# Batch 0's keys as fp32 through SyncE's queue, sums and products in PSUM tiles of their own, and a reordered Y0

## The chip, the cores and the metric

The kernel runs on one core of one Trainium2 chip. The metric is the device time of one launch in microseconds (us), the lower the better. Engines are named as in the profile: PE is TensorE, PEld its weight load, DVE is VectorE, ACT is ScalarE, POOL is GpSimd and SP is SyncE. DMAs are issued by POOL or by SP; the page shows them as queue q0 (software descriptors, from POOL) and q1 (hardware descriptors, from SP and ACT).

## What is computed

Linear attention with the feature map phi(x) = elu(x) + 1, followed by a two-layer block with a swish of learned slope.

```python
# q, k, v: (8 batches, 8 heads, 576 rows, 64), fp32
q_p, k_p = phi(q), phi(k)                      # phi(x) = x > 0 ? x + 1 : exp(x)
kv  = einsum('bhsd,bhse->bhde', k_p, v)
z   = sum(k_p, axis=2)
num = einsum('bhsd,bhde->bhse', q_p, kv)
den = einsum('bhsd,bhd->bhs', q_p, z)[..., None] + 1e-06
x   = (num / den), heads side by side           # 4608 tokens x 512
h   = x @ w_in                                  # w_in 512 x 2048
out = (h / (1 + exp(-beta * h))) @ w_out        # w_out 2048 x 512, out fp32
```

## The kernel before

Each of the 8 batches goes through phi, the products of keys and values, the normalised attention rows x, an H phase (x by w_in, 16 feature blocks, a Silu on ACT after each) and a Y phase (by w_out). A ninth pass takes the rows that the tiles of 512 tokens leave over. PE works through H and Y phases of 16 x 4 matmuls of 512 columns each; the attention of the next batch is woven in between. Only batch 0 has nothing to be woven into: its attention is the head of the kernel. Batch 1's attention is woven into batch 0's Y phase, here called Y0.

One batch of q, k or v is 8 x 576 x 64 numbers, that is 1.18 MB of fp32 in memory. A load by POOL into a bf16 tile casts on the way, so that it writes half as many bytes (576 KB) as it reads. The head:

```python
beta_row = consts.tile([FC, P], F32)
nc.sync.dma_start(out=beta_row, in_=moe_beta...)
nc.vector.memset(warm, 0.5)
nc.scalar.activation(tiny[:, 0:1], warm[:, 0:1], ACTF.Exp)   # brings the table in
for h0 in (0, 2): load(nc.gpsimd, xk[0], k, 0, h0, 2)        # k in two halves, cast to bf16
for h0 in (0, 2): load(nc.gpsimd, xq[0], q, 0, h0, 2)
for h0 in (0, 2): load(nc.gpsimd, vb[0], v, 0, h0, 2)
make_identity(nc, identity)                                  # on POOL
make_identity(nc, ident16)
# ... w_in in 4 loads by POOL; w_out 0 and 1 by SP, held until w_in 1 has landed;
# k, q, v of batch 1 by POOL, held until w_in 3 has landed;
# w_out 2 and 3 by SP into `stage`, held until q of batch 1 has landed
```

A "pair" (pr 0 or 1) is half of the heads, as the two loads bring them. phi is done by pairs: `phi_part` is the exponential on ACT, `phi_relu` is max(x, 0) + 1 on DVE, `phi_min` the minimum of both on DVE. `idle(n)` issues n matmuls of 512 columns on constants whose result is not used; they keep PE busy and its clock up.

```python
phi_step("k", 0, phi_part); phi_step("k", 1, phi_part)
idle(18)
bps = ...; nc.tensor.matmul(bps, beta_row, ident16, is_transpose=True, ...)
phi_step("k", 0, phi_relu); phi_step("k", 0, phi_min)
phi_step("q", 0, phi_part); phi_step("q", 1, phi_part, 0, 4); phi_step("q", 1, phi_part, 4, J)
phi_step("k", 1, phi_relu)
# beta_s, beta_m, beta_c, rbeta: five small DVE instructions
phi_step("k", 1, phi_min)
z_products(0, 0, kvz); idle(8); z_products(0, 1, kvz); idle(5)
phi_step("q", 0, phi_relu); phi_step("q", 0, phi_min)
phi_step("q", 1, phi_relu); phi_step("q", 1, phi_min, 0, 4); phi_step("q", 1, phi_min, 4, J)
q_trans0(0); q_trans0(1)
kv_direct(0, 0, kvz); z_evac(kvz)
for hh in range(2): kv_evac(0, hh, (0,), kvz)
q_trans0(2)
kv_direct(0, 1, kvz)
for hh in range(2): kv_evac(0, hh, (1,), kvz)
# ... denominators, numerators, x and its transposes, then H of batch 0
```

`z_products` sums phi(k) over its rows with 18 matmuls against ones, `kv_direct` makes phi(k) times v with 18 matmuls. Both write into the same two PSUM tiles `kvz`, in which each head has 64 columns of kv and one of z. The evacuations take them from there to SBUF under a mask.

Y0, with batch 1's attention and the start of batch 2's phi woven in:

```python
for i in range(2):
    for t in range(4): y_mm(0, t, i, yps[t])        # groups 0 and 1 of w_out
for pr in range(2): z_products(1, pr, kv1)
w_out_scale(2, 0); z_evac(kv1)                      # w_out 2 to bf16, scaled, four DVE instructions
# loads of q, k and v of batch 2, the first held until w_out 2 has landed
q_trans(1, tiles 0 to 3)
y_mm(0, 0, 2, yps[0]); q_trans(1, tile 4); y_mm(0, 1, 2, yps[1])
for pr in range(2): kv_direct(1, pr, kv1)
w_out_scale(3, 0)
for hh in range(2): kv_evac(1, hh, (0, 1), kv1)
# denominators; then numerators and transposes of x among y_mm(0, 2, 2) ... y_mm(0, 3, 3),
# with batch 2's phi on ACT and DVE between them
```

Of the kernel before, what the change touches and what calls it, by code (L numbers as in the profile page):

```python
# [8 lines left out]
F32 = mybir.dt.float32  # L9
BF16 = mybir.dt.bfloat16  # L10
# [6 lines left out]
def kernel(  # L17
# [10 lines left out]
    nc = tc.nc  # L28
# [44 lines left out]
        for a in vf  # L73
    ]

    def load(eng, dst, src, b, h0=0, n=4):

        rows = src[b].rearrange("h (g j) d -> (h g) (j d)", j=J)
        return eng.dma_start(  # L79
            out=dst[:, h0 : h0 + n].rearrange("p h j d -> p h (j d)"),  # L80
            in_=rows.rearrange("(i p) e -> p i e", p=P)[:, h0 : h0 + n],
        )
# [3 lines left out]


    beta_row = consts.tile([FC, P], F32)
    nc.sync.dma_start(out=beta_row, in_=moe_beta.rearrange("(c p) -> c p", p=P))
    nc.vector.memset(warm, 0.5)  # L90
    tiny = consts.tile([P, 2], BF16)
    nc.scalar.activation(tiny[:, 0:1], warm[:, 0:1], ACTF.Exp)
    for h0 in (0, 2):
        load(nc.gpsimd, xk[0], k, 0, h0, 2)
    for h0 in (0, 2):
        load(nc.gpsimd, xq[0], q, 0, h0, 2)
    for h0 in (0, 2):
        load(nc.gpsimd, vb[0], v, 0, h0, 2)
    identity = consts.tile([P, P], BF16)
    make_identity(nc, identity)  # L100
    ident16 = consts.tile([FC, FC], F32)
    make_identity(nc, ident16)

    w_in_v = moe_w_in.rearrange("(c p) f -> p c f", p=P)
    w_out_v = moe_w_out.rearrange("(c p) m -> p c m", p=P)
# [39 lines left out]
    def phi_part(b, a, pr, x, j0=0, j1=J):  # L145

        if j0 == 0:
            st[b, a, pr, "e"] = work.tile([P, 2, J, D], BF16, tag="e", name="e", bufs=3)
        nc.scalar.activation(st[b, a, pr, "e"][:, :, j0:j1], x[:, :, j0:j1], ACTF.Exp)  # L149
# [6 lines left out]
    def phi_tile(b, a):  # L156
        st[b, a] = work.tile([P, 2, J, P], BF16, tag=f"phi{a}", name=f"phi_{a}")
# [7 lines left out]
        )  # L165

    def xin(b, a, pr):
        return (xk if a == "k" else xq)[b % NX][:, 2 * pr : 2 * pr + 2]

    def v_copy(eng, b, pr):  # L170
# [15 lines left out]
                        start=(j == 0), stop=(j == J - 1), skip_group_check=True,  # L186
                    )

    def kvz_out(ps, pr):
        return ps[:, pr * 2 * EA : (pr + 1) * 2 * EA].rearrange("p (h e) -> p h e", h=2)  # L190

    def z_products(b, pr, ps):

        for j in range(J):
            for hh in range(2):
                r = slice(hh * G, (hh + 1) * G)
                nc.tensor.matmul(
                    kvz_out(ps[hh], pr)[:, :, D : D + 1],
                    st[b, "k"][r, pr, j, :], ones[r, :, None],
                    start=(j == 0), stop=(j == J - 1), skip_group_check=True,  # L200
                )

    def kv_direct(b, pr, ps):
        for j in range(J):
            for hh in range(2):
                r = slice(hh * G, (hh + 1) * G)
                nc.tensor.matmul(
                    kvz_out(ps[hh], pr)[:, :, 0:D],
                    st[b, "k"][r, pr, j, :], vb[b][r, 2 * pr : 2 * pr + 2, j, :],
                    start=(j == 0), stop=(j == J - 1), skip_group_check=True,  # L210
                )

    def kv_evac(b, hh, prs, ps):
        n = len(prs) * 2 * EA
        c = prs[0] * 2 * EA
        nc.vector.tensor_mul(
            st[b, "kv"][:, hh, prs[0] : prs[-1] + 1].rearrange("p a e -> p (a e)"),
            ps[hh][:, c : c + n],
            kvmask.rearrange("p a g e -> p (a g e)")[:, c : c + n],
        )  # L220

    def kv_tile(b):
# [120 lines left out]
    def mm_tile(name):  # L343
        return mmps.tile([P, 512], F32, tag="mm", name=name)

    def y_mm(b, t, i, yp, c0=0, c1=512):
        for c in range(4):
            ff = 4 * i + c
            nc.tensor.matmul(  # L349
                yp[:, c0:c1],  # L350
                g_sb[b % 2][:, ff, t * P : (t + 1) * P],
                w_out_sb[i][:, c, c0:c1],
                start=(ff == 0), stop=(ff == FC - 1), skip_group_check=True,
            )
# [40 lines left out]
    phi_tile(0, "k")  # L395
    phi_tile(0, "q")

    kvz = [mm_tile("kvz") for _ in range(2)]
    dps = mm_tile("dps")

    def misc_bf():
        return miscps.tile([P, 1024], BF16, tag="misc", name="tp")

    def z_evac(ps):
        for hh in range(2):
            nc.vector.tensor_mul(
                z0[:, hh],
                ps[hh][:, 0 : 4 * EA].rearrange("p (a h e) -> p a h e", a=2, h=2)[:, :, :, D],
                kvmask[:, :, :, 0],
            )  # L410
# [36 lines left out]
    def phi_step(a, pr, f, *r):  # L447
        f(0, a, pr, *((xin(0, a, pr),) if f is not phi_min else ()), *r)
# [4 lines left out]

    phi_step("k", 0, phi_part)
    phi_step("k", 1, phi_part)
    idle(18)
    bps = miscps.tile([P, FC], F32, tag="misc", name="bps")
    nc.tensor.matmul(bps, beta_row, ident16, is_transpose=True, start=True, stop=True)
    phi_step("k", 0, phi_relu)
    phi_step("k", 0, phi_min)  # L460
    phi_step("q", 0, phi_part)
    phi_step("q", 1, phi_part, 0, 4)
    phi_step("q", 1, phi_part, 4, J)
    phi_step("k", 1, phi_relu)
    nc.vector.tensor_copy(beta_s, bps)
    nc.vector.tensor_mul(beta_m, beta_s, beta_s)
    nc.vector.tensor_scalar(beta_m, beta_m, TINY * TINY, 2.0 * TINY, ALU.is_lt, ALU.mult)
    nc.vector.tensor_add(beta_c, beta_s, beta_m)
    nc.vector.reciprocal(rbeta, beta_c)
    phi_step("k", 1, phi_min)  # L470
    z_products(0, 0, kvz)
    idle(8)
    z_products(0, 1, kvz)
    idle(5)
    phi_step("q", 0, phi_relu)
    phi_step("q", 0, phi_min)
    phi_step("q", 1, phi_relu)
    phi_step("q", 1, phi_min, 0, 4)
    phi_step("q", 1, phi_min, 4, J)

    def q_trans0(t):
        q_trans(0, (t,), misc_bf()[:, 0 : 512 if t < NT - 1 else 256], (nc.scalar,))

    q_trans0(0)
    q_trans0(1)
    kv_direct(0, 0, kvz)
    z_evac(kvz)
    for hh in range(2):
        kv_evac(0, hh, (0,), kvz)
    q_trans0(2)  # L490
    kv_direct(0, 1, kvz)
    for hh in range(2):
        kv_evac(0, hh, (1,), kvz)
    dens(0, (0, 1), dps)
    recips(0, 2, P, dps)
    q_trans0(3)
# [32 lines left out]
    def w_out_scale(i, n_act):  # L529
        for c in range(4):  # L530
            ff = 4 * i + c
            if c < n_act:
                nc.scalar.mul(w_out_sb[i][:, c, :], w_out_f[i][:, c, :], rbeta[:, ff : ff + 1])
            else:
                nc.vector.tensor_scalar(  # L535
                    w_out_sb[i][:, c, :], w_out_f[i][:, c, :], rbeta[:, ff : ff + 1],
                    None, ALU.mult,
                )
# [10 lines left out]
    kv_tile(1)  # L549
    for pr in range(2):  # L550
        z_products(1, pr, kv1)
    w_out_scale(2, 0)
    z_evac(kv1)
    hold(load(nc.gpsimd, xq[2], q, 2), w_out2_dma)
    load(nc.gpsimd, xk[2], k, 2)
# [1 line left out]

    for ts in ((0, 1), (2, 3)):
        q_trans(1, ts, num0_tile().bitcast(BF16), (nc.scalar, nc.scalar))
    y_mm(0, 0, 2, yps[0])  # L560
    dps1 = num0_tile()
    q_trans(1, (4,), dps1.bitcast(BF16)[:, 512:768], (nc.scalar,))
    y_mm(0, 1, 2, yps[1])
    for pr in range(2):
        kv_direct(1, pr, kv1)
    w_out_scale(3, 0)
    for hh in range(2):
        kv_evac(1, hh, (0, 1), kv1)
# [5 lines left out]
    phi_part(2, "q", 0, xin(2, "q", 0))
    y_mm(0, 2, 2, yps[2])
    numer0(1, 0)
    numer0(1, 1)
    y_mm(0, 3, 2, yps[3])
    x_trans(1, 0, nc.scalar)
    phi_part(2, "q", 1, xin(2, "q", 1))  # L580
    numer0(1, 2)
    y_mm(0, 0, 3, yps[0])
    y_out(0, 0, yps[0])
    x_trans(1, 1, nc.scalar)
# [4 lines left out]
    numer0(1, 3)
    y_mm(0, 1, 3, yps[1])  # L590
    y_out(0, 1, yps[1])
    x_trans(1, 2, nc.scalar)
    phi_min(2, "q", 1)
    phi_part(2, "k", 1, xin(2, "k", 1))
    numer0(1, 4)
    y_mm(0, 2, 3, yps[2])
    y_out(0, 2, yps[2])
    x_trans(1, 3, nc.scalar)
# [91 lines left out]
```

## Time and profile before

| what | value |
|---|---|
| time, median of 3 runs | 297.33 us (296.52 to 297.83) |
| span of the profiled execution | 295.9 us |
| PE busy | 286.0 us, 97% |
| ACT busy | 159.8 us, 54% |
| DVE busy | 116.2 us, 39% |
| POOL busy | 35.2 us, 12% |
| mean granted clock of PE | 1.0 |

PE is counted as busy also in the idle matmuls, so a full PE isn't by itself a useful one: 30 records of them, 9.3 us, stand in the page's groups. The time of the head shows in where the first matmul of H stands, not in PE's share. The rates in GB/s count the bytes that a transfer writes: a casting load that writes 205 GB/s reads 410 GB/s.

### The profile page before, as it was taken

What the parts mean: (1) busy time and instruction counts of PE and PEld (TensorE: products, weight loads), DVE (VectorE), ACT (ScalarE), POOL (GpSimd) and SP (SyncE); (2) the same over time, 40 slices, a digit from 0 to 9 for tenths busy, and PEclk for the clock granted to TensorE, in tenths of its full rate; (3) what the DMA queues carried; (4) which work ended last, traced back from release to release, by engine and by line L of the source; (5) the groups of instructions that cost most, each with busy time, mean ns of one, the idle gap of its engine ahead of it and who ended that gap; (6) DMA issues with size and microseconds to landing.
All of it is one profiled execution on the core that took longest, in us unless ns stands there. A gap on an engine that the chain in (4) does not pass through costs nothing.

```text
span 295.9 us, 4697 instructions
## 1 busy us (share of the span) xinstructions
PE 286.0 (97%) x1855; PEld 143.4 (48%) x1884; DVE 116.2 (39%) x266; ACT 159.8 (54%) x208; POOL 35.2 (12%) x52
## 2 busy tenths in 40 slices
PE   8899989999999999999999999999999999999995
PEld 3484446455445544554455445544554444444443
DVE  3672367944453562265226532553251100110012
ACT  3648873966646790669067906691571068007500
POOL 8302012310022005000500053000000000000000
PEclk9999999999999999999999999999999999999999
DMA  7999999889679939961895189627122310131032
GB/s 89 194 207 337 208 298 172 181 207 223 88 162 283 168 33 231 261 102 40 219 267 97 30 216 263 114 21 177 38 55 50 82 37 0 35 73 35 0 71 74
DMA packets 51911, 40.24 MB, mean 136 GB/s; under 512 B 30752, under 2 KB 42800, under 8 KB 51888
## 3 DMA queue, kind: packets, MB, share of 16 engines
q1 hardware_dynamic: 39536, 26.50, 36.3%
q0 software_dynamic: 12192, 13.31, 27.5%
q8 instruction: 15, 0.25, 0.3%
q10 hardware_dynamic: 160, 0.13, 0.2%
q14 instruction: 8, 0.07, 0.1%
HBM read 36.71 MB, written 9.44 MB: 156 GB/s over the span
## 4 chain that ended last, share of the span: by engine, by line
PE 78%; DMA 14%; POOL 3%; ACT 2%; issue 1%; DVE 0%; SPq 0%; POOLq 0%; ACTq 0%
PE y_ps L349 37%; PE h_ps L331 36%; DMA w_in<-in_moe_w_in_dram 6%; DMA xq<-in_q_dram 5%; PE nps L282 3%; DMA stage<-in_moe_w_out_dram 2%; PE kvp L182 2%; ACT e L149 1%; DMA qTd<-phi_q 1%; POOL xk L79 1%; POOL w_in L107 1%; ACT xT L317 1%; POOL vf L79 0%; POOL xq L79 0%; ACT g L339 0%
## 5 line engine op out<-in xcount | busy, mean ns | idle before, releaser
L339 ACT ACTIVATE g<-h_ps,beta_c 128x512 bf16<-128x512 f32 x144 | 98.5, 688 | 100.1 <-PE h_ps L331 100.1
L349 PE MATMUL y_ps<-w_out,g 128*128 128x512 bf16 (+2 forms) x580 | 126.7, 373 | 2.1 <-DVE w_out L535 1.3
L331 PE MATMUL h_ps<-xT,w_in 128*128 128x512 bf16 (+1 forms) x545 | 116.5, 360 | 0.7 <-ACT xT L317 0.2
L349 PEld LDWEIGHTS <-g 128*128 128x128 bf16 x592 | 57.3, 98 | 66.6 <-issue 2.0
L331 PEld LDWEIGHTS <-w_in 128*128 128x128 bf16 x624 | 56.6, 98 | 58.6 <-issue 0.7
L361 DVE COPY y_sb<-y_ps 128x512 f32<-128x512 f32 (+2 forms) x37 | 24.8, 673 | 83.5 <-PE y_ps L349 78.4
L296 DVE TENSOR_TENSOR xs<-nps,rden 128x512 bf16<-128x512 f32 (+1 forms) x40 | 27.2, 687 | 5.7 <-DMA xT<-xs 3.3
L79 POOL DMA_DIRECT2D xk<-in_k_dram x9 | 7.0, 773 | 119.4 <-DMA qTd<-phi_q 71.9
L149 ACT ACTIVATE e<-xk 128x1152 bf16<-128x1152 bf16 x16 | 17.9, 1152 | 5.2 <-DMA xk<-in_k_dram 5.2
L149 ACT ACTIVATE e<-xq 128x1152 bf16<-128x1152 bf16 (+2 forms) x17 | 18.0, 1099 | 4.4 <-DMA xq<-in_q_dram 4.4
L160 DVE TENSOR_TENSOR phi_q<-e,r 128x1152 bf16<-128x1152 bf16 (+2 forms) x17 | 12.2, 721 | 15.4 <-ACT e L149 15.3
L231 DVE TENSOR_TENSOR kv_bd<-kvp,kvmask 128x260 bf16<-128x260 f32 x12 | 4.6, 423 | 26.4 <-PE kvp L182 26.4
L331 PE MATMUL h_ps<-xT_tail,w_in 128*128 128x512 bf16 x63 | 13.9, 379 | 0.1
L290 DVE TENSOR_SCALAR den<-nps 128x8 f32<-128x8 f32 (+1 forms) x30 | 4.9, 165 | 22.8 <-PE nps L282 22.8
L160 DVE TENSOR_TENSOR phi_k<-e,r 128x1152 bf16<-128x1152 bf16 x16 | 11.5, 748 | 4.1 <-ACT e L149 4.1
L282 PEld LDWEIGHTS <-qTd 128*128 128x128 bf16 x120 | 9.4, 98 | 7.3 <-DMA qTd<-phi_q 0.2
L282 PE MATMUL nps<-kv_bd,qTd 128*128 128x130 bf16 x120 | 12.1, 221 | 0.4
L172 POOL CAST vaug<-vf 128x1152 bf16<-128x1152 f32 x10 | 11.2, 1160 | 4.0 <-DMA vf<-in_v_dram 4.0
L138 PE MATMUL warm_ps<-warm 128*128 128x512 bf16 x30 | 9.3, 474 | 1.6 <-DVE warm L90 1.5
L153 DVE TENSOR_SCALAR r<-xk 128x1152 bf16<-128x1152 bf16 x16 | 7.6, 513 | 5.2 <-DMA xk<-in_k_dram 5.2
L149 ACT ACT_TABLE_LOAD x6 | 7.7, 1283 | 3.5 <-DMA xq<-in_q_dram 3.5
L339 ACT ACT_TABLE_LOAD x7 | 9.0, 1283 | 0.1
(63 smaller groups left out, 101.1 us busy)
## 6 DMA issues: line engine op xcount, KB each, us to landing
out_dram<-y_sb SPq DMA_DIRECT2D x70, 128.0 KB, 2.5
vf<-in_v_dram SPq DMA_DIRECT2D x5, 1152.0 KB, 7.6
xk<-in_k_dram POOLq DMA_DIRECT2D x7, 576.0 KB, 10.0
xq<-in_q_dram POOLq DMA_DIRECT2D x7, 576.0 KB, 12.8
w_in<-in_moe_w_in_dram POOLq DMA_DIRECT2D x4, 512.0 KB, 12.7
g<-in_moe_w_out_dram SPq DMA_DIRECT2D x2, 1024.0 KB, 9.2
stage<-in_moe_w_out_dram SPq DMA_DIRECT2D x2, 1024.0 KB, 8.3
vf<-in_v_dram POOLq DMA_DIRECT2D x2, 576.0 KB, 10.9
```

What stands on the lines that cost most here:

```text
L79: return eng.dma_start(out=dst[:, h0 : h0 + n].rearrange("p h j d -> p h (j d)"), in_=rows.rearrange("(i p) e -> p i e", p=P)[:, h0 : h0 + n],
L138: nc.tensor.matmul(warm_ps[:, 0:cols], warm[:, 0:P], warm[:, 0:cols], start=True, stop=True)
L149: nc.scalar.activation(st[b, a, pr, "e"][:, :, j0:j1], x[:, :, j0:j1], ACTF.Exp)
L153: nc.vector.tensor_scalar(r, x, 0.0, 1.0, ALU.max, ALU.add)
L160: nc.vector.tensor_tensor(st[b, a][:, pr, j0:j1].rearrange("p j (h d) -> p j h d", h=2), st[b, a, pr, "e"][:, :, j0:j1].rearrange("p h j d ...
L172: eng.tensor_copy(vaug[b % 2][:, pr, :, :, 0:D], src[:, 2 * pr : 2 * pr + 2].rearrange("p h j d -> p j h d"),)
L282: nc.tensor.matmul(nps[: qs.shape[-1], hh, pr * 2 * EA : (pr + 1) * 2 * EA], qs, st[b, "kv"][:, hh, pr, :], start=True, stop=True, skip_gr ...
L296: nc.vector.tensor_mul(xs[:n].rearrange("p i a d -> p a i d"), num, rd[:, :, :, None].to_broadcast([n, 2, 4, D]),)
L331: nc.tensor.matmul(hp[:, c0:c1], w_in_sb[ff // 4][:, kc, (ff % 4) * P : (ff % 4 + 1) * P], x[:, kc, c0:c1], start=(kc == 0), stop=(kc == K ...
L339: nc.scalar.activation(g_sb[b % 2][:, ff, :], hp, ACTF.Silu, scale=beta_c[:, ff : ff + 1])
L349: nc.tensor.matmul(yp[:, c0:c1], g_sb[b % 2][:, ff, t * P : (t + 1) * P], w_out_sb[i][:, c, c0:c1], start=(ff == 0), stop=(ff == FC - 1), ...
L361: nc.vector.tensor_copy(y_sb[:, c0:c1], yp[:, c0:c1])
```

## The change

Three parts.

1. Batch 0's k comes by SP's hardware queue, uncast, as fp32, into the space of `stage`, which is free until w_out 2 arrives. It is issued first of all SP's DMAs, ahead of beta. The exponential and the max of k read fp32. POOL makes the two identities first, then loads q, v and w_in. The aim is an earlier start of the data, with the descriptors of k made in a different place from those of q and v.
2. The sums of phi(k) and the two halves of kv are kept in separate PSUM tiles (two tiles for z, two for kv's first pair, two for its second), so that no product waits for an evacuation from the same tile. Idle matmuls become 14 + 4 + 10 in place of 18 + 8 + 5, and the small DVE work on beta stands elsewhere; the reciprocal of beta moves to just before w_out is scaled.
3. In Y0 the kv products of batch 1 come ahead of the third group of Y0, the group which is the first to need w_out 2. Behind it, the numerators and transposes come earlier, two of the eight scalings of w_out 2 and 3 go to ACT, two copies of transposed x go from ACT to DVE, and batch 2's phi comes after batch 1's transposes.

The diff, cut where marked:

```diff
+    k0f = stage[:, 0 : 4 * J * D].rearrange("p (h j d) -> p h j d", h=4, j=J)
@@
+    for h0 in (0, 2):
+        load(nc.sync, k0f, k, 0, h0, 2)
     nc.sync.dma_start(out=beta_row, ...)
     nc.vector.memset(warm, 0.5)
     nc.scalar.activation(tiny[:, 0:1], warm[:, 0:1], ACTF.Exp)
-    for h0 in (0, 2):
-        load(nc.gpsimd, xk[0], k, 0, h0, 2)
+    make_identity(nc, identity)
+    make_identity(nc, ident16)
     # q and v of batch 0, unchanged
-    make_identity(nc, identity)
-    make_identity(nc, ident16)
@@
     def xin(b, a, pr):
+        if b == 0 and a == "k":
+            return k0f[:, 2 * pr : 2 * pr + 2]
@@ z_products, kv_direct, kv_evac: other columns of other tiles; a cut @@
-    kvz = [mm_tile("kvz") for _ in range(2)]
+    kvp0 = [mm_tile("kvp0") for _ in range(2)]
@@
-    idle(18)
-    (transpose of beta)
+    idle(14)
     (phi of k and q: parts)
+    phi_step("k", 1, phi_min)
+    zt = [num0_tile() for _ in range(2)]
+    z_products(0, 0, zt)
+    (transpose of beta)
+    idle(4)
+    z_products(0, 1, zt)
     (beta_s, beta_m, beta_c)
-    nc.vector.reciprocal(rbeta, beta_c)
-    phi_step("k", 1, phi_min)
-    z_products(0, 0, kvz); idle(8); z_products(0, 1, kvz); idle(5)
     phi_step("q", 0, phi_relu)
+    z_evac(zt)
     (the rest of q's phi)
+    idle(10)
     q_trans0(0); q_trans0(1)
-    kv_direct(0, 0, kvz); z_evac(kvz)
-    (kv_evac of pair 0 from kvz)
+    kv_direct(0, 0, kvp0)
+    (kv_evac of pair 0 from kvp0)
     q_trans0(2)
-    kv_direct(0, 1, kvz)
+    kvp1 = [num0_tile() for _ in range(2)]
+    kv_direct(0, 1, kvp1)
@@ Y0 @@
-    w_out_scale(2, 0)            # was ahead of z_evac(kv1)
     q_trans(1, tiles 0 to 3)
-    y_mm(0, 0, 2, yps[0])
+    kv_direct(1, 0, kv1); kv_direct(1, 1, kv1)
+    w_out_scale(2, 0)
+    kv_evac(1, both, kv1)
     q_trans(1, tile 4)
-    y_mm(0, 1, 2, yps[1])
-    kv_direct(1, 0, kv1); kv_direct(1, 1, kv1)
-    w_out_scale(3, 0)
-    kv_evac(1, both, kv1)
+    y_mm(0, 0, 2, yps[0])
     (denominators of batch 1)
-    (batch 2's phi, numerators, x_trans 0 to 3 on ACT, the other y_mm, mixed)
+    y_mm(0, 1, 2, yps[1]); numer0(1, 0); numer0(1, 1)
+    w_out_scale(3, 2)            # two of the four on ACT
+    (y_mm, numerators and x_trans 0, 1 on ACT and 2, 3 on DVE; then batch 2's phi)
```

More of the change, by code (lines that the diff above doesn't have):

```diff
@@ L92 @@
     nc.scalar.activation(tiny[:, 0:1], warm[:, 0:1], ACTF.Exp)
-    for h0 in (0, 2):
-        load(nc.gpsimd, xk[0], k, 0, h0, 2)
+    identity = consts.tile([P, P], BF16)
+    make_identity(nc, identity)
+    ident16 = consts.tile([FC, FC], F32)
+    make_identity(nc, ident16)
     for h0 in (0, 2):
@@ L98 @@
         load(nc.gpsimd, vb[0], v, 0, h0, 2)
-    identity = consts.tile([P, P], BF16)
-    make_identity(nc, identity)
-    ident16 = consts.tile([FC, FC], F32)
-    make_identity(nc, ident16)
     w_in_v = moe_w_in.rearrange("(c p) f -> p c f", p=P)
@@ L187, in kv_products, with row_products @@
                     )
-    def kvz_out(ps, pr):
-        return ps[:, pr * 2 * EA : (pr + 1) * 2 * EA].rearrange("p (h e) -> p h e", h=2)
-    def z_products(b, pr, ps):
+    def row_products(b, pr, dsts, mov):
         for j in range(J):
@@ L197, in z_products, with z_evac @@
                 nc.tensor.matmul(
-                    kvz_out(ps[hh], pr)[:, :, D : D + 1],
-                    st[b, "k"][r, pr, j, :], ones[r, :, None],
+                    dsts[hh], st[b, "k"][r, pr, j, :], mov(r, j),
                     start=(j == 0), stop=(j == J - 1), skip_group_check=True,
                 )
-    def kv_direct(b, pr, ps):
[L204 to L211, printed above, removed]
+    def z_products(b, pr, ps):
+        row_products(b, pr, [a[:, 256 + 2 * pr : 258 + 2 * pr] for a in ps], lambda r, j: ones[r])
+    def z_evac(ps):
+        for hh in range(2):
+            nc.vector.tensor_mul(
+                z0[:, hh], ps[hh][:, 256:260].rearrange("p (a h) -> p a h", a=2),
+                kvmask[:, :, :, 0],
+            )
+    def kv_direct(b, pr, ps):
+        row_products(
+            b, pr, [a[:, pr * P : (pr + 1) * P].rearrange("p (h d) -> p h d", h=2) for a in ps],
+            lambda r, j: vb[b][r, 2 * pr : 2 * pr + 2, j, :],
+        )
     def kv_evac(b, hh, prs, ps):
-        n = len(prs) * 2 * EA
-        c = prs[0] * 2 * EA
+        p0, p1 = prs[0], prs[-1] + 1
         nc.vector.tensor_mul(
-            st[b, "kv"][:, hh, prs[0] : prs[-1] + 1].rearrange("p a e -> p (a e)"),
-            ps[hh][:, c : c + n],
-            kvmask.rearrange("p a g e -> p (a g e)")[:, c : c + n],
+            st[b, "kv"][:, hh, p0:p1].rearrange("p a (h e) -> p a h e", h=2)[:, :, :, 0:D],
+            ps[hh][:, p0 * P : p1 * P].rearrange("p (a h d) -> p a h d", a=p1 - p0, h=2),
+            kvmask[:, p0:p1, :, 0:D],
         )
@@ L402, in misc_bf @@
         return miscps.tile([P, 1024], BF16, tag="misc", name="tp")
[L404 to L410, printed above, removed]
     def dens(b, ts, dps):
@@ L455 @@
     phi_step("k", 1, phi_part)
-    idle(18)
-    bps = miscps.tile([P, FC], F32, tag="misc", name="bps")
-    nc.tensor.matmul(bps, beta_row, ident16, is_transpose=True, start=True, stop=True)
+    idle(14)
     phi_step("k", 0, phi_relu)
@@ L464 @@
     phi_step("k", 1, phi_relu)
+    phi_step("k", 1, phi_min)
+    zt = [num0_tile() for _ in range(2)]
+    z_products(0, 0, zt)
+    bps = miscps.tile([P, FC], F32, tag="misc", name="bps")
+    nc.tensor.matmul(bps, beta_row, ident16, is_transpose=True, start=True, stop=True)
+    idle(4)
+    z_products(0, 1, zt)
     nc.vector.tensor_copy(beta_s, bps)
@@ L468 @@
     nc.vector.tensor_add(beta_c, beta_s, beta_m)
-    nc.vector.reciprocal(rbeta, beta_c)
-    phi_step("k", 1, phi_min)
[L471 to L474, printed above, removed]
     phi_step("q", 0, phi_relu)
+    z_evac(zt)
     phi_step("q", 0, phi_min)
@@ L485 @@
     q_trans0(1)
-    kv_direct(0, 0, kvz)
-    z_evac(kvz)
+    kv_direct(0, 0, kvp0)
     for hh in range(2):
-        kv_evac(0, hh, (0,), kvz)
+        kv_evac(0, hh, (0,), kvp0)
     q_trans0(2)
-    kv_direct(0, 1, kvz)
+    kvp1 = [num0_tile() for _ in range(2)]
+    kv_direct(0, 1, kvp1)
     for hh in range(2):
-        kv_evac(0, hh, (1,), kvz)
+        kv_evac(0, hh, (1,), kvp1)
     dens(0, (0, 1), dps)
@@ L538, in w_out_scale @@
                 )
+    nc.vector.reciprocal(rbeta, beta_c)
     w_out_scale(0, 0)
@@ L559 @@
         q_trans(1, ts, num0_tile().bitcast(BF16), (nc.scalar, nc.scalar))
-    y_mm(0, 0, 2, yps[0])
+    for pr in range(2):
+        kv_direct(1, pr, kv1)
+    w_out_scale(2, 0)
+    for hh in range(2):
+        kv_evac(1, hh, (0, 1), kv1)
     dps1 = num0_tile()
     q_trans(1, (4,), dps1.bitcast(BF16)[:, 512:768], (nc.scalar,))
-    y_mm(0, 1, 2, yps[1])
-    for pr in range(2):
-        kv_direct(1, pr, kv1)
-    w_out_scale(3, 0)
-    for hh in range(2):
-        kv_evac(1, hh, (0, 1), kv1)
+    y_mm(0, 0, 2, yps[0])
     dens(1, range(NT), dps1)
@@ L571 @@
     recips(4, 5, G, dps1)
+    y_mm(0, 1, 2, yps[1])
+    numer0(1, 0)
+    numer0(1, 1)
+    w_out_scale(3, 2)
+    y_mm(0, 2, 2, yps[2])
+    x_trans(1, 0, nc.scalar)
+    numer0(1, 2)
+    y_mm(0, 3, 2, yps[3])
+    x_trans(1, 1, nc.scalar)
+    numer0(1, 3)
+    y_mm(0, 0, 3, yps[0])
+    y_out(0, 0, yps[0])
+    x_trans(1, 2, nc.vector)
+    numer0(1, 4)
+    y_mm(0, 1, 3, yps[1])
+    y_out(0, 1, yps[1])
+    x_trans(1, 3, nc.vector)
     phi_tile(2, "q")
     phi_tile(2, "k")
[L574 to L584, printed above, removed]
+    for pr in range(2):
+        phi_part(2, "q", pr, xin(2, "q", pr))
     for pr in range(2):
@@ L588 @@
     phi_part(2, "k", 0, xin(2, "k", 0))
[L589 to L592, printed above, removed]
+    y_mm(0, 2, 3, yps[2])
+    y_out(0, 2, yps[2])
     phi_min(2, "q", 1)
     phi_part(2, "k", 1, xin(2, "k", 1))
[L595 to L598, printed above, removed]
     y_mm(0, 3, 3, yps[3])
```

## The prediction

> **What bounds the kernel now.** I read the page first: PE's share, then the chain that ended last.
>
> ```profile
> PE 286.0 (97%) x1855; PEld 143.4 (48%) x1884; DVE 116.2 (39%) x266; ACT 159.8 (54%) x208; POOL 35.2 (12%) x52
> ...
> PE 78%; DMA 14%; POOL 3%; ACT 2%; issue 1%; DVE 0%; SPq 0%; POOLq 0%; ACTq 0%
> PE y_ps L349 37%; PE h_ps L331 36%; DMA w_in<-in_moe_w_in_dram 6%; DMA xq<-in_q_dram 5%; PE nps L282 3%; DMA stage<-in_moe_w_out_dram 2%; PE kvp L182 2%; ACT e L149 1%; DMA qTd<-phi_q 1%; POOL xk L79 1%; POOL w_in L107 1%; ACT xT L317 1%; POOL vf L79 0%; POOL xq L79 0%; ACT g L339 0%
> ```
>
> PE is 78% of the chain, in H and Y. The DMA part is 14%, about 41 us, and it lies at the front: the chain by time runs through the loads of w_in, q and w_out up to 49 us and then stays on PE. So there are two parts. From about 56 us on the kernel is PE's, and the change touches nothing there. Before that it is a race between one stream of DMAs and PE. The DMA view of the first 60 us, in 40 slices of 1.5 us, shows the stream:
>
> ```profile
> DMA  0199999999999999999999999899939999997558
> GB/s 0 15 171 185 71 167 194 207 205 205 208 210 204 206 206 295 365 405 383 232 207 205 209 207 207 219 401 314 370 119 104 200 204 208 207 219 215 137 126 204
> ```
>
> It is full from 3 us to about 40 us. Its casting loads write about 207 GB/s, and so read about 414; the uncast loads of w_out write up to 405. Both move the same bytes of memory in the same time, so fp32 instead of bf16 costs the stream nothing. The start is poor, as the windows of 1 us show (the last two numbers are the DMA share and GB/s):
>
> ```profile
> 2.00:3.00 1.00, 1.00 (x4) 0.31 (x3) 0.39 (x4) 0.22 (x2) 1.00 (x3) 1.00 0.24 14
> 3.00:4.00 1.00, 1.00 (x4) 0.31 (x3) 0.00 (x0) 0.00 (x0) 1.00 (x2) 1.00 1.04 152
> 4.00:5.00 1.00, 1.00 (x4) 0.45 (x3) 0.00 (x0) 0.00 (x0) 1.00 (x3) 1.00 1.17 195
> 5.00:6.00 1.00, 1.00 (x4) 0.30 (x2) 0.70 (x1) 0.78 (x1) 1.00 (x2) 1.00 1.23 188
> 6.00:7.00 1.00, 1.00 (x5) 0.44 (x4) 0.58 (x1) 0.39 (x1) 0.86 (x4) 1.00 1.18 75
> 7.00:8.00 1.00, 1.00 (x9) 0.40 (x9) 0.18 (x1) 0.00 (x0) 1.00 (x3) 1.00 0.87 96
> ```
>
> Nothing of size moves before about 2.8 us, though POOL issued k at 1.24, and from 6 to 8 us the rate falls to less than half. At 195 GB/s the hole loses (120 + 99)/195 = 1.1 us of the stream. The timeline shows what the head waits for:
>
> ```profile
> 8.59 1.16 ACT L149 ACTIVATE e<-xk 128x1152 bf16<-128x1152 bf16 x1 [2.21 <-DMA xk<-in_k_dram]
> ...
> 10.02 1.16 ACT L149 ACTIVATE e<-xq 128x1152 bf16<-128x1152 bf16 x1 [0.26 <-DMA xq<-in_q_dram]
> ...
> 12.45 0.87 DVE L160 TENSOR_TENSOR phi_q<-e,r 128x512 bf16<-128x512 bf16 x2
> 12.93 0.34 PEld L250 LDWEIGHTS <-phi_q 128*128 128x128 bf16 x6 [0.70 <-DVE phi_q L160]
> ...
> 18.30 1.05 PE L331 MATMUL h_ps<-xT,w_in 128*128 128x128 bf16 x16
> ...
> 43.51 0.77 PE L349 MATMUL y_ps<-w_out,g 128*128 128x512 bf16 x2 [1.06 <-DVE w_out L535]
> ```
>
> k's halves are usable at 5.2 and 8.6 us, q's from 10.0, q's phi lets PE transpose at 12.9, and H of batch 0 starts at 18.3. From there PE has few holes until Y0's third group waits for w_out 2; in windows of 1 us PE is busy 0.44, 0.47 and 0.78 between 42 and 45 us, so 1.3 us are lost there.
>
> **What the Trainium skill says.** "DMA: Bandwidth & Descriptors", section "SWDGE vs HWDGE vs iDMA": a cast is done only by GpSimd's queue, SP's can't. So k has to stay fp32 there, as the change does it. Its "Specifications" give a first byte after some 1 us for GpSimd's path and some 0.6 us for SP's. The trace agrees in direction: k is issued at 1.24 and moves from about 2.8; beta, issued by SP at 0.74, has bytes in the window 1 to 2 us and lands 1.6 us after its issue.
>
> "SBUF — State Buffer", section "SBUF: two separate sides": a DVE instruction in a two-port mode locks GpSimd out of its port, and a DMA by GpSimd then lacks descriptors, while SP's is immune. The hole at 6 to 8 us follows the first DVE work on k (5.22, 0.70 us, against 0.46 for the second of its kind) and POOL's making of the identities (5.64 to 7.23). I can't tell from this trace which of them made it.
>
> "VectorE: DVE Perf Modes", section "Mode 2×_2P": with one fp32 source in SBUF it makes two elements a cycle, where bf16 may reach four. The trace has a scaling of w_out, 512 fp32 elements, in 0.42 to 0.48 us; less about 0.15 us of fixed time, 1152 of them should take about 0.75 us, an estimate. Per pair of k that is 0.3 us more than 0.46. ACT's exponential takes 1.16 us for 1152 elements, and I take the same for fp32 (no fp32 exponential is in this trace).
>
> **Part 1: k by SP.** SP starts at 0.74 as it did for beta, so data from about 1.5 instead of 2.8 us: 1.3 us gained by the whole stream, as what follows is queued behind. q is still issued by POOL at about 2.8, since the identities (0.43 + 0.29 + 0.10 + 0.68 = 1.5 us) now take the place of k's two issues (1.55 us). Its packets start at about 4.4, when k's second half is ending. If the hole goes too, another 1.1 us is gained, plus what uneven engines lose in it: q's first half would land at 6.4 us (1.5, plus k and half of q, 1.77 MB at 410 GB/s = 4.3, plus 0.5 to be seen), against 10.0. If it stays, about 8.5. I give the two even chances, mean 7.4, and with it the stream ahead by 1.5 to 3.5 us.
>
> What the head makes of it is less, as DVE becomes the limit. Estimate, with k at 3.6 and 5.1: relu and min of pair 0 to 5.6, relu (0.75) and min (0.70) of pair 1 to 7.1. Beta's copy needs PE, which has 14 idle matmuls (cold 0.43 us each up to about 6.1, then 0.21) and the first sums to do: 7.6. Four beta instructions at 0.2: 8.4. relu of q 8.9, the z evacuations 9.2, min 9.9, relu 10.4, two min's of 0.44: 11.2. Before they ended at 13.3. So 2.1 us are gained without the hole, about 1.4 with it. PE arrives at the q transposes when 4 idle matmuls (0.86), the second sums (0.38) and 10 idle ones (2.1) are done, about 10.8: they just fit.
>
> **Part 2: own PSUM tiles.** The second kv half waited 0.19 us for an evacuation of the first; that and z's earlier evacuation are worth 0.2 to 0.3 us on this path. Sum for the start of H: 18.3 less about 2.0 = **16.3 us**. w_in 0 landed at 16.9 before, 9.7 us after its issue; with the stream ahead by 1.5 to 3.5 it is there by 13.4 to 15.4. w_out 0 and 1 (landed 27.8 and 30.4) are needed at 31.8 instead of 33.8, and come early too.
>
> **Part 3: Y0.** Before, PE finished its q transposes at 42.45 and waited for w_out 2 (landed 42.9, first scaling 0.5 later). After, everything up to there is 2.0 earlier, so 40.4; then 36 kv matmuls, 1.2 us, bring it to 41.6. w_out 2 lands at 42.9 less 1.5 to 3.5 = 39.4 to 41.4, its first quarter is scaled at 39.9 to 41.9. The wait is closed, or nearly so, and of the 1.3 us of hole about **1.0** is won. The numerators no longer stand behind four scalings of w_out 3 in DVE's queue (1.7 us), which keeps PE fed. Batch 2's phi, later on ACT, costs nothing I can find: its four exponentials (4.6 us) and a table load (1.28) end some 2 us after H of batch 1 begins, but PE has four PSUM tiles, 3.5 us of work, before it needs the first Silu.
>
> Sum: 2.0 + 1.0 = 3.0 us, and H of batch 1 starts at about 52.9 instead of 55.9. From there on 240 us of PE work are as before and shifted. 297.3 - 3.0 = **294.3 us**.
>
> **Rivals.** (1) *DVE or PE's idle matmuls take the place of the DMA.* The five phi and beta steps of DVE leave no gap by my count, and the ten idle matmuls sit right ahead of the transposes; each half microsecond that z's sums come later goes straight into the start of H. For it: DVE was busy 3.65 of 5 us from 10 to 15. It would halve the gain of part 1: 295.5. (2) *The stream stays as late as before*: SP's loads of k are slow at the start, or share with q so that q doesn't gain; then only 0.5 us comes from the head, and part 3 gives little, since w_out 2 is as late as ever: 296.5. Against it: SP's loads of w_out run at 365 to 405 GB/s. (3) *Given back later*: batch 2's transposed q (landed 64.7, with PE waiting 0.22 for it) and its products hang on loads held behind w_out 2 and on DVE, which was busy 5.0 of 5 us from 55 to 60. If they don't move with PE, H of batch 1 waits for them and 1 to 2 us are lost: 295.5 to 296. (4) *The hole goes and more holes close*: the head gains 3, Y0 1.5: 292.5.
>
> **Range and chances.** The middle is between the main reckoning and the rivals on its slow side, 294.4 us. The best case, (4), a little exceeded, sets the low end, 292.2; (2) with the spread of runs (0.5 us) the high end, 297.0. A gain over 2% needs 291.4 us, 6 us off a head in which the stream can give 3.5 and Y0 1.3: 0.03. A loss over 2% needs a new wait of 6 us in a part where nothing is added to PE: 0.02.
>
> **What would show it.** Step by step in the profile after: the first exponential of k at 3.6 to 4.2 us, and the second at about 5.2 to 5.5; relu of k at 0.75 us; no hole in GB/s at 6 to 8 us if the descriptors were its cause and are not disturbed anew; first exponential of q at 6.5 to 8.5; the first H matmul at 16.3; PE without a wait for w_out 2 at 41 to 43; H of batch 1 at 52.9; and from there equal lengths. It is wrong if the exponential of k waits beyond 5 us, if H of batch 0 starts after 17.5, or if the stretch from H of batch 1 to the end is longer by more than 0.5 us than before.

## The result and the profile after

| | before | changed |
|---|---|---|
| time, median of 4 runs | 297.51 us | 332.63 us |
| lowest to highest | 296.52 to 297.83 | 332.10 to 333.71 |
| ratio of the times | 1 | 1.119 (95% interval 1.115 to 1.123) |
| span of the profiled execution | 295.9 us | 330.5 us |
| mean granted clock of PE | 1.0 | 0.936 |

The changed kernel is 12% slower, where 1% faster was predicted. The page says at a glance where: these are PE, granted clock, DMA and rate over 40 slices of 8.3 us, and the busy totals.

```profile
PE 286.1 (87%) x1853; PEld 143.3 (43%) x1881; DVE 115.2 (35%) x266; ACT 159.3 (48%) x208; POOL 32.9 (10%) x50
...
PE   6000079999999999999999999999999999999995
...
PEclk9555559999999999999999999999999999999999
DMA  8999994000279679679918942991522221022013
GB/s 197 205 269 263 289 181 73 2 1 2 49 162 259 90 181 267 109 83 279 175 25 203 267 82 65 251 209 43 134 66 50 56 65 32 0 63 65 0 43 85
```

PE is busy for as long as before (286.1 and 286.0 us), so nothing was added to its work. From slice 2 to slice 5, about 8 to 41 us, it does nothing at all, and its clock is at 0.5 from there to slice 6. Meanwhile the loads run on, until at about 49 us nothing is left to move. The waits of the first 96 us name the cause (engine and line, what it waited for, us in total, times, longest):

```profile
ACT e L151 <- DMA stage<-in_moe_w_out_dram: 40.4, 2, 38.3
DVE r L155 <- DMA stage<-in_moe_w_out_dram: 39.4, 2, 38.1
PEld L197 <- DVE phi_k L162: 38.4, 2, 36.6
PE nps L197 <- DVE phi_k L162: 37.0, 2, 36.2
```

The exponential and the max of batch 0's *k* wait for a load of *w_out*. The timeline shows it with the times:

```profile
0.74 0.97 SPq L81 DMA_DIRECT2D stage<-in_k_dram  x2
...
34.35 0.92 SPq L114 DMA_DIRECT2D stage<-in_moe_w_out_dram  x2
40.55 1.16 ACT L151 ACTIVATE e<-stage 128x1152 bf16<-128x1152 f32 x1 [38.32 <-DMA stage<-in_moe_w_out_dram]
...
42.57 0.40 PE L197 MATMUL nps<-ones,phi_k 64*128 64x2 bf16 x18 [36.15 <-DVE phi_k L162]
...
43.80 1.16 ACT L151 ACTIVATE e<-stage 128x1152 bf16<-128x1152 f32 x1 [2.09 <-DMA stage<-in_moe_w_out_dram]
```

k was issued at 0.74 us, and its two loads landed 3.6 and 4.8 us after their issue. But k lies in `stage`, and `stage` is also where w_out 2 and 3 go. In the program text the two lines that load w_out 2 and 3 stand near the top, ahead of the lines of phi. A reader waits for the last writer ahead of it in the text. For k's readers that is not k's load but w_out's, which is itself held until q of batch 1 has landed. So the head of the kernel starts at 40.55 us, when w_out 2 is there, and its second pair at 43.80, when w_out 3 is.

It must also be said what is read then. w_out 2 covers columns 0 to 2047 of `stage`, w_out 3 the columns behind them, and k columns 0 to 2303, with its second pair from 1152 on. So, by these times, phi is taken of w_out's numbers in k's place from 40.55 us on, and what becomes batch 0's attention isn't that of its k. The same holds for experiments 4 and 5 below. The instructions and their shapes are the same ones, so the time can be read as the time of this order of waits.

Where the 34.6 us of span come from, by the first matmul of each H phase in the two timelines:

| stretch | before, us | changed, us | difference |
|---|---|---|---|
| start to H of batch 0 | 18.30 | 54.97 | +36.67 |
| H of batch 0 to H of batch 1 | 37.61 | 35.20 | -2.41 |
| H of batch 1 to the end | 240.0 | 240.3 | +0.3 |

All of the loss, and more, is in the head. Between the two H phases 2.41 us are won, and behind them the kernel is 0.3 us longer than before.

### The profile page after: what moved, and what is told of

It is laid out like the page before. It is cut to its first block, busy times and chain, and to the rows that moved or that the text cites. A ratio compares the mean times of both kernels' runs of the same rounds, so it can differ in the third digit from the quotient of the medians.

```text
span 330.5 us, 4700 instructions
## 1 busy us (share of the span) xinstructions
PE 286.1 (87%) x1853; PEld 143.3 (43%) x1881; DVE 115.2 (35%) x266; ACT 159.3 (48%) x208; POOL 32.9 (10%) x50
## 4 chain that ended last, share of the span: by engine, by line
PE 81%; DMA 12%; POOL 2%; ACT 2%; issue 1%; DVE 1%; SPq 0%; POOLq 0%; ACTq 0%
PE y_ps L354 37%; PE h_ps L336 35%; DMA w_in<-in_moe_w_in_dram 5%; DMA stage<-in_moe_w_out_dram 3%; DMA xq<-in_q_dram 3%; PE nps L287 2%; PE kvp L186 2%; DMA qTd<-phi_q 1%; PE warm_ps L140 1%; PE nps L434 1%; ACT g L344 1%; POOL w_in L109 1%; PE xtp L317 1%; PE kv L197 0%; POOL xq L81 0%
## 5 line engine op out<-in xcount | busy, mean ns | idle before, releaser
L197 PE MATMUL nps<-ones,phi_k 64*128 64x2 bf16 x36 | 0.8, 164 | 37.0 <-DVE phi_k L162 37.0
L151 ACT ACTIVATE e<-stage 128x1152 bf16<-128x1152 f32 x2 | 2.3, 1163 | 40.4 <-DMA stage<-in_moe_w_out_dram 40.4
L81 POOL DMA_DIRECT2D xk<-in_k_dram x7 | 5.2, 746 | 152.3 <-DMA qTd<-phi_q 134.9
L197 PEld LDWEIGHTS <-phi_k 64*128 64x128 bf16 x144 | 3.2, 96 | 39.1 <-DVE phi_k L162 38.4
L162 DVE TENSOR_TENSOR phi_q<-e,r 128x1152 bf16<-128x1152 bf16 (+2 forms) x17 | 12.1, 721 | 15.3 <-ACT e L151 15.2
L151 ACT ACTIVATE e<-xk 128x1152 bf16<-128x1152 bf16 x14 | 15.5, 1150 | 1.4 <-DVE phi_q L162 1.4
L155 DVE TENSOR_SCALAR r<-stage 128x1152 bf16<-128x1152 f32 x2 | 1.5, 760 | 39.4 <-DMA stage<-in_moe_w_out_dram 39.4
L140 PE MATMUL warm_ps<-warm 128*128 128x512 bf16 x27 | 10.4, 557 | 1.8 <-DVE warm L94 1.5
```

The source lines that it names most:

```text
L81: return eng.dma_start(out=dst[:, h0 : h0 + n].rearrange("p h j d -> p h (j d)"), in_=rows.rearrange("(i p) e -> p i e", p=P)[:, h0 : h0 + n],
L140: nc.tensor.matmul(warm_ps[:, 0:cols], warm[:, 0:P], warm[:, 0:cols], start=True, stop=True)
L162: nc.vector.tensor_tensor(st[b, a][:, pr, j0:j1].rearrange("p j (h d) -> p j h d", h=2), st[b, a, pr, "e"][:, :, j0:j1].rearrange("p h j d ...
```

## The experiments

The theory (A): the order of the text against the shared space, and nothing else. Its rivals: B, k by SP's queue or fp32 reads are slow in themselves; C, the clock is a cause, not a consequence.

**1. The loads of w_out 2 and 3 behind k's readers.** Ratios here and below are against the kernel before on the same chip.

```diff
     load(nc.gpsimd, vb[1], v, 1)
-    w_out2_dma = load_w_out(2, q1_dma)
-    load_w_out(3)
@@
     phi_step("k", 1, phi_relu)
+    w_out2_dma = load_w_out(2, q1_dma)
+    load_w_out(3)
     phi_step("k", 1, phi_min)
```

> The changed kernel with one edit: the two lines that load w_out 2 and w_out 3 into the shared space stage are put behind batch 0's exponential and max of k in the program text. The order of SP's queue stays as it is; only the order against the readers of k changes. Theory A (the text order makes k's readers wait for w_out 2 and 3, 40.55 and 43.8 us): the first exponential of k starts at 4.0 to 5.0 us, H of batch 0 near 16.5, H of batch 1 near 53, time 293 to 296 us. Rival B (k by SP's queue or fp32 reads are slow in themselves): above 320 us. Rival C (the clock: it falls to 0.5 from 8 us on for a reason other than PE's wait): the clock falls again and the time stays above 305 us.

Measured: 294.77 us, ratio 0.991 (0.988 to 0.994). Two lines, moved in the text without a change of SP's own order, are worth 38 us. The timeline of this version:

```profile
4.34 1.17 ACT L149 ACTIVATE e<-stage 128x1152 bf16<-128x1152 f32 x1 [2.11 <-DMA stage<-in_k_dram]
...
6.07 1.16 ACT L149 ACTIVATE e<-stage 128x1152 bf16<-128x1152 f32 x1 [0.56 <-DMA stage<-in_k_dram]
...
8.05 1.16 ACT L149 ACTIVATE e<-xq 128x1152 bf16<-128x1152 bf16 x1 [0.81 <-DMA xq<-in_q_dram]
...
9.55 1.26 ACT L149 ACTIVATE e<-xq 128x512 bf16<-128x512 bf16 x2 [0.33 <-DMA xq<-in_q_dram]
...
15.92 1.05 PE L334 MATMUL h_ps<-xT,w_in 128*128 128x128 bf16 x16
```

The reader now waits for `in_k`, at 4.34 us. B falls: k by SP, as fp32, is early. C falls in the form in which it was put for this run: the mean granted clock is 0.999.

**2. k in another space, the text order left alone.**

```diff
-    k0f = stage[:, 0 : 4 * J * D]...
+    k0f = g_sb[0]... .bitcast(F32)[:, 0 : 4 * J * D]...   # written first by batch 0's first Silu
```

> The changed kernel with one edit: the fp32 k lies in the space of g of batch 0 (which is first written by the first Silu of batch 0) instead of in stage. Text order and queue order as in the changed kernel. Theory A: no wait for w_out, the same as with the loads put later within 1 us, 293 to 296 us. Rival B or C: above 305 us. If it differs from the run with the loads put later by over 1 us, the order of the text has another effect than the wait.

Measured: 294.95 us, ratio 0.991 (0.988 to 0.994), H of batch 0 at 16.17. The first exponential waits for k's own load:

```profile
4.19 1.16 ACT L151 ACTIVATE e<-g 128x1152 bf16<-128x1152 f32 x1 [1.96 <-DMA g<-in_k_dram]
```

Either end of the clash can be taken away, order or space, with the same result. So it is their meeting that costs.

**3. The wait alone, put into the kernel before.**

```diff
-        nc.scalar.activation(e, x, ACTF.Exp)
+        d = nc.scalar.activation(e, x, ACTF.Exp)
+        if b == 0 and a == "k":
+            hold(d, w_out23[pr])          # the load of w_out 2 for pair 0, of w_out 3 for pair 1
```

> The kernel before with one thing added: the exponentials of batch 0's k wait for the loads of w_out 2 (first pair) and w_out 3 (second pair); k still comes by POOL as bf16 to its own tile. Nothing else of the change is in it. Theory A: the first exponential starts at 43.0 us and the second at about 46, H of batch 0 at 56 to 57, the wait for w_out 2 in Y0 (1.3 us) is gone, time about 334 us (331 to 337). Rivals B and C: SP's queue and fp32 aren't in it, so 298 to 300.

Measured: 332.78 us, ratio 1.118 (1.114 to 1.123), 0.15 us from the changed kernel and within its spread. k comes here by POOL, as bf16, to its own tile:

```profile
41.97 1.16 ACT L149 ACTIVATE e<-xk 128x1152 bf16<-128x1152 bf16 x1 [39.73 <-DMA stage<-in_moe_w_out_dram]
...
44.72 1.16 ACT L149 ACTIVATE e<-xk 128x1152 bf16<-128x1152 bf16 x1 [1.59 <-DMA stage<-in_moe_w_out_dram]
```

The wait is not only necessary for the loss but enough for it. I had expected the two about 1 us later: w_out 2 landed at 41.9 in this execution and not at 42.9. H of batch 0, expected at 56 to 57, came at 54.77.

**4. The same wait, for less time.** The changed kernel with w_out loaded in the order 2, 3, 0, 1, held only until w_in 1 has landed; k's readers still behind it in the text.

```diff
-    load_w_out(0, w_in_dma[1])
+    w_out2_dma = load_w_out(2, w_in_dma[1])
+    load_w_out(3)
+    load_w_out(0)
     load_w_out(1)
@@
-    w_out2_dma = load_w_out(2, q1_dma)
-    load_w_out(3)
```

> The changed kernel with SP's loads of w_out in the order 2, 3, 0, 1, all held only until w_in 1 has landed (17.9 us). k's readers still stand behind w_out 2 and 3 in the text. Theory A: the head starts when these two have landed, near 26 and 28 us in place of 40.55 and 43.8, H of batch 0 near 39.5 in place of 55.0, time about 317 us (315 to 319). Rivals B and C, for which the order of w_out plays no part: 332.

Measured: 317.46 us, ratio 1.067 (1.063 to 1.071). k's exponentials start at 26.44 and 29.15, H of batch 0 at 39.77:

```profile
26.44 1.16 ACT L151 ACTIVATE e<-stage 128x1152 bf16<-128x1152 f32 x1 [24.21 <-DMA stage<-in_moe_w_out_dram]
...
29.15 1.16 ACT L151 ACTIVATE e<-stage 128x1152 bf16<-128x1152 f32 x1 [1.54 <-DMA stage<-in_moe_w_out_dram]
```

The head begins 14.1 us earlier than in the changed kernel, and the time is 15.2 us shorter. The loss follows the landing of w_out 2 and 3.

**5. PE kept busy through the wait.** The changed kernel with `idle(14)` replaced by `idle(176)`.

> The changed kernel with 176 idle matmuls in place of the first 14, so that PE stays busy and its clock up until k's readers are released at 40.6 us. Question: how much of the 35 us is the clock, which is at 0.5 from 8 to 50 us in the changed kernel. Theory A (the wait is nearly all; the clock only stretches the 10 idle matmuls ahead of the q transposes, which start at 49.9 although q's phi was ready at 48.6): H of batch 0 at 53.5 to 54.2 instead of 54.97, time 331 to 332. Rival C (the clock is a main part of the loss): 326 or less.

Measured: 332.53 us, ratio 1.115 (1.106 to 1.125), from two executions of 331.00 and 334.05 us. The changed kernel lies inside that interval. This is the window of 6 to 40.5 us (PE busy first, granted clock third from the end):

```profile
6.00:40.50 34.50, 34.34 (x159) 15.64 (x160) 0.00 (x0) 0.00 (x0) 3.82 (x6) 1.00 1.15 243
```

34 us at full clock instead of half of it don't bring 326 us or less: C falls as a main cause. The gain of about 1 us that I had expected for theory A isn't seen, and the run can't measure it. Its interval is 2.9 us wide to either side, and the trace is of the longer execution: w_out 2 came 0.9 us later in it (first exponential at 41.48), and H of batch 0 stood at 56.71, where 53.5 to 54.2 was expected. Besides, PE idles 2.31 us before the first sums and 1.45 us before the second ones; after the second gap the clock is at 0.5 again, and the ten idle matmuls ahead of the q transposes are cold as before. So the clock's own share isn't measured. From the second release of k to H of batch 0 the changed kernel takes 11.17 us (43.80 to 54.97) and experiment 1 takes 9.85 (6.07 to 15.92). The difference, 1.3 us, is an estimate of what is lost behind the wait, with the matmuls at half clock in it; it is a low one, as experiment 1 still waits for q in that stretch.

**6 to 8. The parts, with the order mended.** Each alone, or with one part left out, all measured side by side.

Parts 1 and 2 without Y0's reorder (the version of experiment 1, with the Y0 block of the kernel before):

> The version with the loads of w_out 2 and 3 put later, but with Y0 as in the kernel before (parts 1 and 2 without part 3). From that version's profile: H of batch 0 at 15.9 again (18.3 before). Theory: Y0 then waits for w_out 2 as before, which lands 2.2 us earlier, so H of batch 1 comes at about 53.7 and the time is about 295.5 (294.8 to 296.3). Rival: the head's gain goes on in full and Y0's reorder is worth nothing: 294.8, the same as with it. Rival 2: the head's gain is lost in the wait for w_out 2: 297.

Part 3 alone (the kernel before, with the Y0 block of the changed kernel):

> The kernel before with Y0 as in the changed kernel (part 3 alone). H of batch 0 at 18.3 as before. With the loads put later the stretch from H of batch 0 to H of batch 1 took 36.0 us against 37.6, so theory: 1.3 to 1.6 us less, about 296.2 (295.7 to 296.8). Rival: without the earlier stream w_out 2 comes too late for it and nothing is gained: 297.6.

Part 1 alone (the kernel before, with `k0f`, its two loads by SP, the identities first and w_out 2 and 3 loaded behind k's readers):

> The kernel before with batch 0's k by SP as fp32 into stage, the identities first, and w_out 2 and 3 loaded behind k's readers; PSUM tiles, idle matmuls (18, 8, 5), beta's work and Y0 as before (part 1 alone). Theory: q lands at 8.05 as in the version with all three parts, H of batch 0 at 16.2 to 16.6, H of batch 1 held by w_out 2 near 53.8, time 295.6 (295.0 to 296.5). Rival: the old idle matmuls and shared tiles eat the gain, 297.

In this table "q" is the start of the exponentials of q's second load; "rest" is the stretch from H of batch 1 to the end of the span.

| | time, us | ratio, 95% interval | q, us | H of batch 0, us | H of batch 1, us | rest, us |
|---|---|---|---|---|---|---|
| before (first trace) | 297.45 | 1 | 11.54 | 18.30 | 55.91 | 240.0 |
| part 1 alone | 296.20 | 0.996 (0.994 to 0.998) | 10.27 | 17.05 | 53.55 | 240.0 |
| parts 1 and 2 | 297.46 | 0.999 (0.997 to 1.001) | 9.75 | 16.12 | 53.54 | 239.8 |
| part 3 alone | 296.58 | 0.996 (0.994 to 0.998) | 11.37 | 18.07 | 53.28 | 241.2 |
| all three (experiment 1) | 294.77 | 0.991 (0.988 to 0.994) | 9.55 | 15.92 | 51.96 | 240.7 |
| all three, k in g (experiment 2) | 294.95 | 0.991 (0.988 to 0.994) | 9.81 | 16.17 | 52.93 | 240.6 |
| all three again (experiment 10) | 295.25 | 0.993 (0.990 to 0.996) | 9.92 | 16.29 | 52.86 | 241.6 |

Part 1 and part 3 bring 0.4% each, with times inside the ranges given for them, and all three together 0.7 to 0.9%. Single traces must be read with care: experiments 1 and 10 are the same kernel, and their H phases of batch 0 and 1 stand 0.4 and 0.9 us apart.

The head follows q. From the exponentials of q's second load to H of batch 0 it is 6.36 to 6.37 us in all four traces with part 2, and 6.70 to 6.78 in the three without it. So part 2 is worth 0.3 to 0.4 us. This is part 1 alone, beside the lines of experiment 1 above:

```profile
10.27 1.26 ACT L149 ACTIVATE e<-xq 128x512 bf16<-128x512 bf16 x2 [0.34 <-DMA xq<-in_q_dram]
...
17.05 1.05 PE L333 MATMUL h_ps<-xT,w_in 128*128 128x128 bf16 x16
```

The other 0.5 us between 17.05 and 16.12 is an earlier landing of q in that execution. Nothing of either reaches H of batch 1 (53.55 and 53.54). The wait lines of PE in Y0 tell why. This one is of part 1 alone (us in total, times, longest):

```profile
PE y_ps L351 <- DVE w_out L539: 0.2, 1, 0.2
```

And this one is of parts 1 and 2:

```profile
PE y_ps L352 <- DVE w_out L533: 1.1, 2, 0.9
```

The 0.9 us by which the head is earlier are waited away for w_out 2. The 2.4 us against the kernel before are not, so the second rival of that run, which put the time at 297, is near the measured time, but the trace, with its span of 293.3 us, doesn't bear it out. What isn't settled is why parts 1 and 2 measure 297.46: in 11 of its 20 executions (3 and 1 of 20 for part 1 and part 3 alone) the mean granted clock was 0.988 to 0.994 and the median 298.2 us, in the other 9, at 0.998 or above, it was 296.0, and the trace is of one of these 9, so that where the clock dipped can't be read.

With part 3, which does batch 1's kv products in this place, H of batch 1 comes at 51.96 to 52.93 when the head is early, and PE still waits 0.2, 0.9 and 0.7 us for w_out 2 (experiments 1, 2 and 10). Part 3 also gives something back: the rest takes 240.6 to 241.6 us with it and 239.8 to 240.0 without. These are waits of PE behind H of batch 1, in experiment 10:

```profile
PE h_ps L334 <- DVE y_sb L364: 0.9, 1, 0.9
PE nps L285 <- DMA qTd<-phi_q: 0.7, 1, 0.7
```

The first is for a copy of Y0's output, the second for batch 2's transposed q. Alone, against the kernel before, part 3 is a gain. That it adds one to parts 1 and 2 the traces don't show: their spans are 292.7, 293.5 and 294.5 us with it, and 293.3 without.

**9 and 10. An attempt at more: q by SP as well.** The version of experiment 1, with batch 0's q as fp32 behind k and beta on SP's queue into the space of g of batch 0, and 5 idle matmuls ahead of the q transposes in place of 10; beside it experiment 1 again.

```diff
+    q0f = g_sb[0]... .bitcast(F32)[:, 0 : 4 * J * D]...
@@
     nc.sync.dma_start(out=beta_row, ...)
+    for h0 in (0, 2):
+        load(nc.sync, q0f, q, 0, h0, 2)
-    for h0 in (0, 2):
-        load(nc.gpsimd, xq[0], q, 0, h0, 2)
@@
-    idle(10)
+    idle(5)
```

> A version meant to be faster: the one with the loads of w_out 2 and 3 put later, and in addition batch 0's q by SP as fp32 as well, behind k and beta, into the space of g of batch 0; POOL starts with v; 5 idle matmuls in place of 10 ahead of the q transposes. In the version without this POOL's queue moved nothing before 5 us although q was issued at 1.61, and q was usable at 8.05 and 9.55. Theory A (the stream's gap between SP's and POOL's queue goes to a place where nobody waits): q usable at 7.0 to 7.4 and 8.5 to 8.9, H of batch 0 at 15.0 to 15.4 instead of 15.9, time 294.0, or unchanged at 294.8 if w_out 2 then is what Y0 waits for. Rival: max and exponential of q in fp32 and beta's later landing cost more than is won, 295.5. POOL's first bytes (v) tell if its queue stands still while SP's moves: then they come after 7.5 us, and at about 3.2 if not.

> The version with the loads of w_out 2 and 3 put later once more, unchanged, for a comparison with the one above on the same chip: 294.8, within 0.6.

Measured: 300.30 us with q by SP, ratio 1.011 (1.006 to 1.016); 295.25 us for experiment 1 again, ratio 0.993 (0.990 to 0.996). q became usable at 10.46 and 13.38 instead of 8.05 and 9.55, later even than in the kernel before (10.02 and 11.54):

```profile
10.46 1.16 ACT L152 ACTIVATE e<-g 128x1152 bf16<-128x1152 f32 x1 [3.29 <-DMA g<-in_q_dram]
```

The queues of the window of 9 to 10 us say why (packets, MB, share of 16 engines):

```profile
q0 software_dynamic: 92, 0.10, 57.9%
q1 hardware_dynamic: 89, 0.18, 52.8%
```

POOL had issued v and w_in from 1.6 us on, and from 7 to 12 us both queues moved packets in nearly equal numbers (76 and 77 in the first of these windows of 1 us, 95 and 85 in the last). In one queue q had gone ahead of v; in two it goes beside it, and gets half. PE then ran dry at 9.8 us but for two transposes, and its clock was at 0.5 from 13 to 19.7 us, with most of the head's matmuls in it:

```profile
12.00:13.00 1.00, 0.29 (x2) 0.11 (x2) 0.42 (x1) 0.00 (x0) 0.00 (x0) 0.94 1.22 239
13.00:14.00 1.00, 0.00 (x0) 0.00 (x0) 0.62 (x1) 0.56 (x2) 0.00 (x0) 0.50 1.22 204
```

H of batch 0 came at 21.70, which is 5.8 us later than in experiment 1. Of this, 3.9 us are q's second load (exponentials at 13.44 instead of 9.55); the other 1.9 lie behind it, where the matmuls ran at half clock. So the version with the order mended (experiment 1) stays the best: 294.77 and 295.25 us in two measurements, against 297.77 and 297.65 for the kernel before beside it.

## Why the prediction was wrong, point by point

**The step that failed.** It is in "Part 1: k by SP": "Estimate, with k at 3.6 and 5.1". It takes the landing of k as the moment from which k can be read. The landing was nearly right: in experiment 1 the first exponentials start at 4.34 and 6.07 us, 0.1 and 0.6 us behind the ranges "3.6 to 4.2 us, and the second at about 5.2 to 5.5". The release was not: in the changed kernel k's readers were let go at 40.55 and 43.80 us, by w_out 2 and w_out 3. The prediction took over from "The change" that `stage` is free until w_out 2 arrives, and names no dependence between k and w_out 2. Which of the two waits for the other is set by the order of the text, and there the load comes first. So k's readers wait, and the load doesn't wait for them. The text itself shows this without a run: `load_w_out(2, q1_dma)` and `load_w_out(3)` write `stage`, and stand ahead of the first `phi_step`. No rival had a wait that turns round in this way. The prediction did say that a loss over 2% "needs a new wait of 6 us", and gave it 0.02; that wait came, with 36 us. It also named the sign that came true, an exponential of k that "waits beyond 5 us". Experiments 1 to 4 show the cause from four sides.

**The other steps**, measured where the order is mended (experiments 1, 2 and 10), since there the whole rest of the reckoning is to be seen:

- *Data from about 1.5 us.* k's first packets moved between 1.8 and 2.0 us. Beta's, from which the 1.5 was taken, had moved between 1.6 and 2.4 us in the kernel before.
- *fp32 costs the stream nothing, relu of k 0.75 us.* Right for the stream: 394 GB/s written between 3 and 4 us. The second relu took 0.75 to 0.76 us, the first 0.85, 1.00 and 0.87, where in the changed kernel, at 40.57 us, it took 0.76; why isn't known. The exponential of fp32 took 1.16 to 1.17 us as the bf16 one did.
- *The hole at 6 to 8 us: even chances to go.* In between. It is a dip at 5 to 7 us now, 142 and 181 GB/s instead of 75 and 96. The starvation of POOL's descriptors that the Trainium skill states ("SBUF — State Buffer", section "SBUF: two separate sides") wasn't tested here, and which of the candidates made the hole stays open.
- *q's packets start at about 4.4.* They started between 5.0 and 5.5 us, though POOL issued q earlier than I thought, at 1.61 (the identities took 0.9 us and not 1.5). q was usable at 8.05 to 8.44, within the 6.4 to 8.5 given. (The terms of the 6.4 add up to 6.3.)
- *H of batch 0 at 16.3, part 2 worth 0.2 to 0.3 us.* Right: 15.92 to 16.29, and part 2 is worth 0.3 to 0.4 us.
- *The wait for w_out 2 closed, 1.0 us won.* In part: PE's wait fell from 1.3 us to 0.2, 0.9 and 0.7, and the stretch from H to H from 37.6 to 36.0, 36.8 and 36.6.
- *H of batch 1 at 52.9, then 240 us as before.* 51.96, 52.93 and 52.86, then 240.6 to 241.6. The third rival was right in part: 0.6 to 1.6 us are given back, for batch 2's transposed q (0.5 to 0.7 us) and, in experiment 10, for a copy of Y0's output. The prediction's own mark for this, 0.5 us, is passed, so "the change touches nothing there" doesn't hold behind 56 us.
- *294.3 us, range 292.2 to 297.0.* 294.77, 294.95 and 295.25.

So the reckoning of the gain held within 1 us, with its last two terms only in part, and the loss came from a premise that no step of it had checked.

## What to carry to other kernels

Where a space is used twice, ask for each reader which writer stands last ahead of it in the program text, not which lands first; a load lifted to the top of the text, harmless while its space has one use, becomes the release of every reader behind it. For the first instruction that a change is to make earlier, list everything that it waits for before reckoning with the arrival of its data. And a gain in the head counts only as far as the next load that PE meets: with parts 1 and 2, H of batch 0 stood 0.9 us earlier than with part 1, and H of batch 1 stood where it was.

## What the runs showed of the hardware that I had not expected

- Once its clock was at 0.5, PE got the full clock back only after a stretch of nearly unbroken matmuls: 2.9 us in the changed kernel (46.55 to 49.4), 5.0 us with q by SP (14.7 to 19.7), 5.3 us in experiment 5 (47.2 to 52.5). Keeping PE busy for 34 us of a wait was of no visible use there: behind two later gaps of 2.31 and 1.45 us the clock was at 0.5 again.
- POOL's loads moved nothing before 5.0 us in experiment 1, where SP had issued k first. That is 3.4 us after POOL's first issue at 1.61; in the kernel before it was about 1.55 us. SP's two loads of k were moving in that time, with 187 packets of q1 and none of q0 between 3 and 4 us. Whether POOL's queue stood behind k or was late for another reason isn't settled: with q by SP too, POOL's bytes also began at 5.0 to 5.5 us, with SP's queue still at work, and neither at 3.2 nor after 7.5 us as the two readings of that run had it.
